# Delta-rule attention feeding a rational MLP: two products of the block inverse and the state's second half on Pool, the second half of the off-diagonal blocks on ACT and PE

## The chip, the cores and the metric

The kernel runs on one core of one Trainium2 chip. The metric is the device time of one launch in microseconds; the kernel before takes 858.86 us, the median of three runs (855.03 to 863.0).

A core has five engines that run their own instruction streams in order and meet at semaphores. In the profile, PE is TensorE (matrix products, results in PSUM; PEld is its weight load), DVE is VectorE, ACT is ScalarE, POOL is GpSimd, and SP is the engine that issues nearly all of this kernel's DMAs.

## The reference, cut to what matters

```python
# delta rule, per batch and head (4 x 8), over 768 tokens of head width 48
k_n = k / (norm(k) + 1e-6)
for t in range(S):
    y[t]  = q[t] @ state
    v_old = k_n[t] @ state
    state = state + beta[t] * outer(k_n[t], v[t] - v_old)
# the 3072 rows of y (8 heads x 48 = 384 wide) then go through an MLP of width 2048
h = x @ w_in
P = a0 + a1*h + a2*h**2 + a3*h**3
Q = 1 + |b0|*|h| + |b1|*h**2
out = (P / (Q + 1e-6)) @ w_out
```

All inputs and the output are float32 (moe_w_in and moe_w_out are float64 and are read as pairs of words).

## The kernel before

**Chunks.** The 768 tokens are cut into 12 chunks of 64. Within a chunk the sequential rule becomes matrix products: the 64x64 matrix of key products, its strictly lower part times beta, a triangular solve against it, one product for the state's update and one for the output. Two batches lie side by side on the 128 partitions, so a tile is 128 partitions by 16 (batch pair, head) combinations by 48 or 64 columns: 768 or 1024 elements per partition.

**Two halves.** Every product on PE runs in float16 with each operand split into a first half (the value rounded to float16) and a second half (the rest, again float16). `split16` makes them: ACT writes the first half, DVE or POOL subtracts it from the source. `mm3` then makes three passes, first by first, second by first, first by second, 48 matrix products in all for the 16 heads.

**The inverse (lines 526 to 594).** The triangular matrix is cut into 16x16 diagonal blocks, which are inverted with elementwise instructions, 128 blocks on 128 partitions at once. It begins with 4x4 blocks, and a loop then joins two 4x4 into 8x8 (n = 4) and two 8x8 into 16x16 (n = 8). Each join is a product of blocks written as an elementwise product (line 564), a sum over the last axis (line 567), a second product (line 569) and a second sum (line 574). For n = 8 each product has 512 elements per partition; for n = 4 there are two of 64. The inverse, times 256, is split into two halves (lines 580 and 581, both on DVE) and goes through DRAM (`img`) to the layout that PE needs (`wc`). There is one buffer of the inverse (`wt`); its diagonal is written by ACT in line 537.

**The off-diagonal blocks (lines 596 to 609).** PE multiplies the key products by the inverse of the diagonal blocks into a PSUM tile `pe`. `split16` makes the two halves of pe / 256 in `et`: ACT the first, DVE the second, from PSUM. Six SP transfers a chunk lay them out as block-diagonal weights `ebd`. The solve (lines 685 to 701) is a product with `wbd` and three steps with `ebd`, each with a split of its own.

**The state (lines 667 to 683 and 703 to 712).** `S16` is the state in float32, updated by DVE in line 708. `state_split` makes its two halves `sh`, scaled by d["ss"]: ACT the first (line 230), DVE the second (line 234). `residual` multiplies the keys with `sh` on PE into `pk`, and DVE subtracts that from v in line 679.

**The MLP.** A chunk's 256 tokens go through the MLP in eight units of 256 hidden columns, 96 units in all. In each, PE makes `ph` (18 products, line 806); ACT, DVE and POOL make numerator, denominator and quotient (lines 823 to 853; ACT takes a logarithm and an exponential to divide, and POOL writes the quotient's second half `mg` in line 853); and PE adds the unit's part of the output in `po` (12 products, line 868).

**The order.** At the start, a list of letters ("fgbwoafagfa") runs through the first chunks' stages, and the weights are loaded, converted from float64 and split. In the main loop, each of a chunk's eight units carries pieces of the attention of later chunks: the solve, state and outputs one chunk ahead (`back`), off-diagonal blocks, state split and residual two ahead (`middle`), key products, inverse and query products three ahead (`front`), loads four ahead (`ahead`). The code's order isn't the final order: a planner simulates the engines with modelled costs and arranges the instructions by that, and `tc.high_priority` lets the solve, the off-diagonal blocks, the state split and the residual go earlier.

**Buffers.** `pe` lies in a PSUM pool with one buffer, which key and query products (`pg`, `pm`) also use. The tag "fq" is one SBUF buffer for the squares of keys, queries and values (lines 464 and 616).

Of the kernel before, what the change touches and what calls it, by code (L numbers as in the profile page):

```python
# [10 lines left out]
F16 = mybir.dt.float16  # L11
F32 = mybir.dt.float32
BF16 = mybir.dt.bfloat16
U32 = mybir.dt.uint32
AF = mybir.ActivationFunctionType
ALU = mybir.AluOpType
# [20 lines left out]
def kernel(  # L37
# [12 lines left out]
    nc = tc.nc  # L50

    B, H, S, D = q.shape
    DM, DFF = moe_w_in.shape
    P = 128
    C = 64
# [7 lines left out]
    HP = NPAIR * H  # L63
# [16 lines left out]
    cpool = ctx.enter_context(tc.tile_pool(name="cpool", bufs=1))  # L80
    sb = ctx.enter_context(tc.tile_pool(name="sb", bufs=2))
# [10 lines left out]
    PAIRS = range(NPAIR)  # L92
# [4 lines left out]
    def mark(nm, c, dma):  # L97
        marks[f"{nm}{c}"] = dma.ins
# [24 lines left out]
    identf = cpool.tile([P, P], F32, name="identf")  # L123
    make_identity(nc, identf)
    ident16 = cpool.tile([P, P], F16, name="ident16")
    nc.vector.tensor_copy(ident16, identf)

    zmask = cpool.tile([P, NB], F32, name="zmask")
    nc.vector.tensor_reduce(
# [5 lines left out]
    nc.gpsimd.memset(ones16, 1.0)  # L135


    mask = cpool.tile([P, C], F32, name="mask")
    nc.gpsimd.memset(mask, 1.0 / 256.0)
    for b in range(2):  # L140
        sl = slice(b * C, (b + 1) * C)
# [34 lines left out]
    def zeroed(n, shape, dtype, nm, part=lambda t: t, eng=nc.gpsimd):  # L176
        made = []
        for i in range(n):
# [14 lines left out]
            eng=nc.vector if nm in "kwe" else nc.gpsimd,  # L193
# [10 lines left out]
    for i in range(NIMG):  # L204
        t = dfix.tile([P, BS], F32, name=f"img{i}")
# [3 lines left out]
    def as_rows(ap, b):  # L209

        return (
            ap[b * C : (b + 1) * C]
            .rearrange("(m j) x -> m (j x)", j=NB)[:, : C * C]
            .rearrange("m (t s) -> t m s", s=C)
        )

    def as_blocks(ap):

        return ap[:, : 16 * C].rearrange("m (i s) -> m i s", s=C)[:, :, :16]

    S16 = cpool.tile([P, HP, D], F32, name="S16")

    def split16(dst, src, scale=None, eng=None, hi=None):

        if hi is not None:
            hi.tensor_scalar(dst[0], src, 1.0 if scale is None else scale, 0.0, op0=ALU.mult, op1=ALU.add)
        elif scale is None:
            nc.scalar.copy(dst[0], src)  # L228
        else:
            nc.scalar.activation(dst[0], src, AF.Copy, scale=scale)  # L230
        if scale is None:
            (eng or nc.vector).tensor_sub(dst[1], src, dst[0])  # L232
        else:
            nc.vector.scalar_tensor_tensor(  # L234
                out=dst[1], in0=src, scalar=scale, in1=dst[0], op0=ALU.mult, op1=ALU.subtract
            )

    def parts(t):
        return t[:, 0], t[:, 1]
# [155 lines left out]
    def mm3(dst, bd, rt, start=True, stop=True):  # L395

        for p in PAIRS:
            mm3p(dst, bd, rt, p, start, stop)
# [13 lines left out]
    def bank(pool, nm, w):  # L412

        t = pool.tile([P, NPAIR, 512], F32, tag="a", name=nm)[:, :, : H * w].rearrange("x p (h w) -> x p h w", w=w)
        return t[:, 0], t[:, 1], t

    def by_pair(t):

        return t.rearrange("x (p h) d -> x p h d", p=NPAIR)

    def parts_by_pair(t):
        return by_pair(t[:, 0]), by_pair(t[:, 1])
# [103 lines left out]
    def inverse(c):  # L526


        d = info[c]
        gb = sb.tile([P, 272], F32, tag="gb", name=f"gb_{c}", bufs=1)  # L530
        dma = nc.sync.dma_start(out=gb[:, :256].rearrange("p (i j) -> p i j", j=16), in_=as_blocks(d.pop("gd")))
        mark("gb", c, dma)
        yield
        wt = wt_b[0]
        pr = sb.tile([P, 512], F32, tag="pr", name=f"pr_{c}", bufs=1)
        xt = sb.tile([P, 64], F32, tag="ab", name=f"ab_{c}", bufs=1)
        nc.scalar.copy(wt[:, 0:256:17], bblk[:, c])

        def blocks(t, n, at, x):

            t = t.rearrange("p (e x) -> p e x", x=x)[:, :, at : at + 16 * n]
            return t.rearrange("p e (i j) -> p e i j", j=16)[..., :n]


        w4 = blocks(wt, 4, 0, 68)
        a4 = xt.rearrange("p (e i j) -> p e i j", e=4, i=4)
        b4 = bblk[:, c].rearrange("p (e i) -> p e i", e=4)
        nc.vector.tensor_mul(a4, blocks(gb, 4, 0, 68), b4.unsqueeze(3).broadcast_to([P, 4, 4, 4]))
        for i in range(1, 4):
            pv = pr[:, : 4 * i * i].rearrange("p (e k j) -> p e k j", e=4, k=i)  # L550
            ai = a4[:, :, i, :i].unsqueeze(2).broadcast_to([P, 4, i, i])
            nc.vector.tensor_mul(pv, w4[:, :, :i, :i], ai)
            nc.vector.tensor_reduce(w4[:, :, :i, i], pv, axis=AX.X, op=ALU.add)

        for n in (4, 8):
            x = 34 * n
            e = 8 // n
            shape = [P, n, n, n]
            w21 = blocks(wt, n, n, x)
            prod = pr[:, : e * n ** 3].rearrange("p (e a b j) -> p e a b j", e=e, a=n, b=n)  # L560
            xs = xt[:, : e * n * n].rearrange("p (e i j) -> p e i j", e=e, i=n)
            g21, w11, w22 = blocks(gb, n, 16 * n, x), blocks(wt, n, 0, x), blocks(wt, n, 17 * n, x)
            for m in range(e):
                nc.vector.tensor_mul(
                    prod[:, m], g21[:, m].unsqueeze(1).broadcast_to(shape), w11[:, m].unsqueeze(2).broadcast_to(shape)
                )
            nc.vector.tensor_reduce(xs, prod, axis=AX.X, op=ALU.add)
            for m in range(e):
                nc.vector.tensor_mul(
                    prod[:, m],  # L570
                    xs[:, m].unsqueeze(2).broadcast_to(shape),
                    w22[:, m].rearrange("p k i -> p i k").unsqueeze(1).broadcast_to(shape),
                )
            nc.vector.tensor_reduce(w21, prod, axis=AX.X, op=ALU.add)
            if n == 4:
                yield
        wtf = wt[:, :256]

        wh = sb.tile([P, 256, 2], F16, tag="wh", name=f"wh_{c}", bufs=1)
        nc.vector.tensor_scalar_mul(wh[..., 0], wtf, 256.0)  # L580
        nc.vector.scalar_tensor_tensor(
            out=wh[..., 1], in0=wtf, scalar=256.0, in1=wh[..., 0], op0=ALU.mult, op1=ALU.subtract
        )
        if c == 0:
            nc.vector.tensor_scalar(
                gate.bitcast(U32), wtf[:, 127:128].bitcast(U32), 0, 897 << 20, op0=ALU.bitwise_and, op1=ALU.bitwise_or
            )
        im = img[c % NIMG]
        words = wh.rearrange("p x i -> p (x i)").bitcast(F32)
        nc.sync.dma_start(out=as_blocks(im), in_=words.rearrange("m (t c) -> m t c", c=16))  # L590
        wc = d["wc"] = sb.tile([P, HP, C, 2], F16, tag="wc", name=f"wc_{c}", bufs=1)
        words = wc.rearrange("p m s i -> p (m s i)").bitcast(F32).rearrange("p (m s) -> p m s", s=C)
        for b in range(2):
            nc.sync.dma_start(out=words[b * C : (b + 1) * C], in_=as_rows(im, b))

    def off_blocks(c):

        d = info[c]
        gbd, wc = d.pop("gbd"), d.pop("wc")
        pe = bank(ps_f, f"pe_{c}", C - 16)  # L600
        mm3(pe, gbd, wc[:, :, 16:])
        d["wbd"] = to_diagonal("w", wc)
        et = sb.tile([P, 2, HP, C - 16], F16, tag="u0", name=f"et_{c}", bufs=1)
        split16(parts_by_pair(et), pe[2], 1.0 / 256.0)
        ebd = d["ebd"] = diag["e"][0]
        for b in range(2):
            for j in range(NB - 1):
                sl = slice(b * C + 16 * j, b * C + 16 * j + 16)
                nc.sync.dma_start(out=ebd[sl, :, :, b, 16 * (j + 1) :], in_=et[sl, :, :, 16 * j :])
# [57 lines left out]
    def state_split(c):  # L667

        d = info[c]
        d["sh"] = sb.tile([P, 2, HP, D], F16, tag="sh", name=f"sh_{c}", bufs=2)  # L670
        split16(parts(d["sh"]), S16, d["ss"])

    def residual(c):
        d = info[c]
# [263 lines left out]
    def middle(c, j):  # L938

        if j == 0:  # L940
            with tc.high_priority(1000):
                info[c]["gbd"] = to_diagonal("w", info[c].pop("gl"))
        elif j == 3:
            with tc.high_priority(300):
                off_blocks(c)
        elif j == 5:
            if c > 0:
                with tc.high_priority(300):
                    state_split(c)
            with tc.high_priority(300):  # L950
                residual(c)
            diagonals(c)
# [53 lines left out]
    for n in range(N + 2):  # L1006
        c, j = divmod(n, NU)
# [38 lines left out]
```

## Time and profile before

| what | value |
|---|---|
| median of 3 runs | 858.86 us (855.03 to 863.0) |
| the profiled execution, its own time | 857.44 us |
| its span, first to last instruction | 855.5 us |
| mean granted TensorE clock | 0.883 |
| instructions | 23235 |

| engine | busy us | share | instructions |
|---|---|---|---|
| PE | 624.5 | 73% | 9264 |
| DVE | 770.2 | 90% | 1369 |
| ACT | 593.4 | 69% | 1242 |
| POOL | 467.6 | 55% | 430 |

How to read the rows that follow. A row of instruction groups gives the line of the code, the engine, the operation, the tile written and the tiles read, the form (partitions by elements, types) and the count; behind the first bar the busy time in us and the mean duration of one in ns; behind the second the time in us that the engine stood idle just before these instructions, and what ended most of it. A row by stage gives the stretch in us from the span's start and then each engine's busy time, with the count of instructions. A row of waits names who waited for whom: us in total, how often, the longest. In a row of one line's durations stand shortest, median and longest in ns, and then the first and last start in us. A line can be that of a helper: 234 and 230 are in `split16`, 403 is in `mm3p`, so the tile's name tells which use it is. PE's busy time is modelled for pipelined products and isn't its peak rate.

### The profile page before, as it was taken

Reading aid. Unit: us, or ns where it says so; the run is one execution under the profiler, and the core shown is the slowest. Engines: PE = TensorE matmul, PEld = TensorE weight load, DVE = VectorE, ACT = ScalarE, POOL = GpSimd, SP = SyncE. Lnnn points to the kernel's source line nnn. Section 1 sums busy time; section 2 is a strip of 40 time slices with the busy share of each in tenths; the row PEclk is TensorE's granted clock in tenths of the full one; section 3 lists DMA queues with packets and bytes.
Section 4 is the critical chain, followed back from the end, with each engine's and each line's share of the span. In section 5 each row is a group of like instructions: output and inputs, shape, how many; then the busy total and the mean of one; then the engine's idle time right before and its main releaser. Section 6 shows DMA issues by size and latency. Waiting matters only on the chain. (4 is left out here: it accounts for less than half of the span.)

```text
span 855.5 us, 23235 instructions
## 1 busy us (share of the span) xinstructions
PE 624.5 (73%) x9264; PEld 491.8 (57%) x9264; DVE 770.2 (90%) x1369; ACT 593.4 (69%) x1242; POOL 467.6 (55%) x430
## 2 busy tenths in 40 slices
PE   0230425865887697598878979888789889999885
PEld 0220424644666376476667757666677667776563
DVE  5999898899889969889899999998999998998896
ACT  4766666865666584685867777767768767887774
POOL 7665655454436345654764855746738455353622
PEclk9755555987899799889989999999989999999998
DMA  8997979966996976878879779579588572300000
GB/s 236 245 202 155 221 148 173 143 137 131 162 158 112 182 142 112 143 148 154 145 139 162 118 147 165 102 148 162 97 169 143 114 114 49 71 2 20 1 19 19
DMA packets 466508, 111.47 MB, mean 130 GB/s; under 512 B 431328, under 2 KB 463072, under 8 KB 466400
## 3 DMA queue, kind: packets, MB, share of 16 engines
q1 hardware_dynamic: 464224, 108.83, 68.5%
q8 instruction: 72, 1.18, 0.6%
q10 hardware_dynamic: 2176, 1.17, 0.4%
q14 instruction: 36, 0.29, 0.1%
HBM read 40.47 MB, written 26.23 MB: 78 GB/s over the span
## 5 line engine op out<-in xcount | busy, mean ns | idle before, releaser
L806 PE MATMUL ph<-xT,w_in 128*128 128x256 f16 x1728 | 225.6, 285 | 39.2 <-DVE mu L830 32.8
L868 PE MATMUL po<-w_out,mg 128*128 128x384 f16 x1152 | 219.0, 337 | 35.0 <-POOL mg L853 31.4
L806 PEld LDWEIGHTS <-w_in 128*128 128x128 f16 x1728 | 173.1, 102 | 76.7 <-DVE mu L830 34.9
L853 POOL TENSOR_TENSOR mg<-mu,mr 128x512 f16<-128x512 f32 x96 | 133.5, 1391 | 132.7 <-DVE mu L852 83.2
L868 PEld LDWEIGHTS <-mg 128*128 128x128 f16 x1152 | 109.3, 100 | 109.7 <-POOL mg L853 41.0
L823 ACT ACTIVATE mu<-ph,coef,msc 128x512 f32<-128x512 f32 x96 | 74.0, 771 | 49.4 <-POOL mg L853 20.2
L829 ACT ACTIVATE mw<-mw 128x512 f32<-128x512 f32 x96 | 60.4, 629 | 55.3 <-DVE mw L828 55.0
L848 DVE SCALAR_TENSOR_TENSOR mw<-mw,msc,mg 128x512 f32<-128x512 f32 x96 | 87.0, 907 | 0.7
L826 DVE TENSOR_TENSOR mu<-ph,mu 128x512 f32<-128x512 f32 x96 | 65.4, 681 | 19.4 <-ACT mr L825 14.0
L850 POOL TENSOR_TENSOR mu<-mu,mw 128x512 f32<-128x512 f32 x36 | 50.3, 1398 | 53.1 <-DVE mw L848 31.2
L403 PEld LDWEIGHTS <-kbd 128*128 128x128 f16 x1680 | 59.8, 102 | 25.5 <-issue 19.1
L828 DVE SCALAR_TENSOR_TENSOR mw<-mr,msc,ph 128x512 f32<-128x512 f32 x96 | 70.5, 735 | 0.0
L830 DVE SCALAR_TENSOR_TENSOR mu<-mu,msc,ph 128x512 f32<-128x512 f32 x96 | 70.4, 734 | 0.0
L841 ACT ACTIVATE mr<-mw,msc 128x512 f32<-128x512 f32 x96 | 69.0, 719 | 1.2
L403 PE MATMUL pu<-z,ebd 128*128 128x48 f16 x1728 | 53.7, 186 | 20.3 <-DVE z L234 14.9
L403 PEld LDWEIGHTS <-ebd 128*128 128x128 f16 x1728 | 52.8, 98 | 22.8 <-issue 21.5
L825 ACT ACTIVATE mr<-ph,msc 128x512 f32<-128x512 f32 x96 | 65.2, 679 | 0.0
L847 DVE SCALAR_TENSOR_TENSOR mg<-mu,msc,mr 128x512 f16<-128x512 f32 x60 | 59.3, 988 | 2.5 <-ACT mr L842 2.5
L842 ACT ACTIVATE mr<-mr 128x512 f32<-128x512 f32 x96 | 60.0, 625 | 1.1
L852 DVE SCALAR_TENSOR_TENSOR mu<-mu,msc,mw 128x512 f32<-128x512 f32 x60 | 55.7, 928 | 0.4
L403 PEld LDWEIGHTS <-wbd 128*128 128x128 f16 x1152 | 38.6, 101 | 28.3 <-issue 27.1
L232 POOL TENSOR_TENSOR mm<-m,mm 128x1024 f16<-128x1024 f32 x12 | 31.7, 2639 | 34.2 <-ACT mm L228 34.2
(198 smaller groups left out, 1313.7 us busy)
## 6 DMA issues: line engine op xcount, KB each, us to landing
wsi<-in_moe_w_in_dram SPq DMA_DIRECT2D x24, 256.0 KB, 5.2
xdk<-kn SPq DMA_DIRECT2D x24, 256.0 KB, 3.6
kbd<-tk SPq DMA_DIRECT2D x24, 256.0 KB, 4.5
gd<-g SPq DMA_DIRECT2D x24, 256.0 KB, 3.8
wso<-in_moe_w_out_dram SPq DMA_DIRECT2D x32, 192.0 KB, 3.8
xdq<-kn SPq DMA_DIRECT2D x24, 256.0 KB, 3.4
mbd<-mm SPq DMA_DIRECT2D x24, 256.0 KB, 5.8
wc<-img SPq DMA_DIRECT2D x24, 256.0 KB, 5.3
```

Of the source, the lines that this page charges most:

```text
L403: nc.tensor.matmul(dst[p][:, h], head(bd, lp, p * H + h), head(rt, rp, p * H + h), start=start and n == 0 and h == 0, stop=stop and n == l ...
L806: nc.tensor.matmul(ph[:, i], w_in[:, f2, wp, cc, i * P : (i + 1) * P], x[:, xp, cc], start=k == 0, stop=k == 3 * NCC - 1,)
L823: nc.scalar.activation(u, ph, AF.Identity, scale=A3, bias=a2)
L825: nc.scalar.activation(z, ph, AF.Abs, scale=B1)
L826: nc.vector.tensor_mul(u, ph, u)
L828: nc.vector.scalar_tensor_tensor(out=w, in0=z, scalar=B0, in1=ph, op0=ALU.add, op1=ALU.mult)
L829: nc.scalar.activation(w, w, AF.Abs)
L830: nc.vector.scalar_tensor_tensor(out=u, in0=u, scalar=A1, in1=ph, op0=ALU.add, op1=ALU.mult)
L841: nc.scalar.activation(r, w, AF.Ln, bias=Q0)
L848: nc.vector.scalar_tensor_tensor(out=w, in0=w, scalar=Q0, in1=g[:, 0], op0=ALU.add, op1=ALU.mult)
L853: nc.gpsimd.tensor_mul(g[:, 1], u, r)
L868: nc.tensor.matmul(po[p], g[:, gp, i, p * P : (p + 1) * P], w_out[:, f2, wp, i], start=f2 == lo and i == 0 and k == 0, stop=f2 == hi - 1 a ...
```

## The change

1. The two elementwise products of the inverse go from DVE to POOL for n = 8 (two of 512 elements a chunk); for n = 4 they stay on DVE, as do all sums.
2. The inverse's first half (`wh`, line 580) is made by ACT instead of DVE.
3. In the off-diagonal blocks, ACT writes the first half as before; PE then adds -256 times that half to `pe`, as a product with a constant matrix (-256 on the diagonal), one for each of the two batch pairs; and ACT scales what is left by 1/256 into the second half. The DVE instruction goes.
4. The state's second half: ACT writes the scaled state to a float32 tile `st` (in the buffer "fq"), and POOL subtracts the first half from it. The DVE instruction goes.
5. A new constant tile `minus256`, made once; the causal mask (0 and 1/256) becomes bfloat16.

```diff
@@ constants
+    minus256 = cpool.tile([P, P], F16, name="minus256")
+    nc.vector.tensor_scalar(minus256, identf, -256.0, None, op0=ALU.mult)
-    mask = cpool.tile([P, C], F32, name="mask")
+    mask = cpool.tile([P, C], BF16, name="mask")
@@ inverse
+            eng = nc.vector if n == 4 else nc.gpsimd
             for m in range(e):
-                nc.vector.tensor_mul(
+                eng.tensor_mul(
                     prod[:, m], g21[:, m].unsqueeze(1).broadcast_to(shape), w11[:, m].unsqueeze(2).broadcast_to(shape)
                 )
             nc.vector.tensor_reduce(xs, prod, axis=AX.X, op=ALU.add)
             for m in range(e):
-                nc.vector.tensor_mul(
+                eng.tensor_mul(
                     prod[:, m],
                     xs[:, m].unsqueeze(2).broadcast_to(shape),
                     w22[:, m].rearrange("p k i -> p i k").unsqueeze(1).broadcast_to(shape),
...
-        nc.vector.tensor_scalar_mul(wh[..., 0], wtf, 256.0)
+        nc.scalar.activation(wh[..., 0], wtf, AF.Copy, scale=256.0)
@@ off_blocks
-        split16(parts_by_pair(et), pe[2], 1.0 / 256.0)
+
+        for i in range(2):
+            nc.scalar.activation(parts_by_pair(et)[i], pe[2], AF.Copy, scale=1.0 / 256.0)
+            for p in PAIRS if i == 0 else ():
+                nc.tensor.matmul(
+                    pe[p].rearrange("x h t -> x (h t)"),
+                    minus256,
+                    et[:, 0, p * H : (p + 1) * H].rearrange("x h t -> x (h t)"),
+                    start=False,
+                    stop=True,
+                    skip_group_check=True,
+                )
@@ state_split
-        split16(parts(d["sh"]), S16, d["ss"])
+        hi, lo = parts(d["sh"])
+        nc.scalar.activation(hi, S16, AF.Copy, scale=d["ss"])
+        st = sb.tile([P, HP, D], F32, tag="fq", name=f"st_{c}", bufs=1)
+        nc.scalar.activation(st, S16, AF.Copy, scale=d["ss"])
+        nc.gpsimd.tensor_sub(lo, st, hi)
```

## The prediction, on record before the result

> **What bounds the kernel now.** I read the page first (busy shares, slices), then busy time by stage, then the waits, then the costs of the forms that the change touches.
>
> ```profile
> span 855.5 us, 23235 instructions
> ...
> PE 624.5 (73%) x9264; PEld 491.8 (57%) x9264; DVE 770.2 (90%) x1369; ACT 593.4 (69%) x1242; POOL 467.6 (55%) x430
> ...
> DVE  5999898899889969889899999998999998998896
> ```
>
> DVE is busy 90% of the span, and its slices are 8 or 9 nearly everywhere. By stage:
>
> ```profile
> core 0: us, PE busy (x) PEld busy (x) DVE busy (x) ACT busy (x) POOL busy (x), PEclk, DMA share, GB/s
> 160.00:250.00 90.00, 62.22 (x908) 47.52 (x905) 85.41 (x144) 58.74 (x127) 44.03 (x35) 0.87 0.78 143
> 250.00:400.00 150.00, 117.06 (x1927) 94.04 (x1928) 129.21 (x213) 96.69 (x193) 75.64 (x66) 0.90 0.79 144
> 400.00:600.00 200.00, 169.96 (x2661) 134.87 (x2658) 187.25 (x303) 148.38 (x296) 125.16 (x100) 0.96 0.83 144
> ...
> sum 695.00, PE 571.75 PEld 445.82 DVE 631.94 ACT 489.64 POOL 371.58; mean PE 114.35 PEld 89.16 DVE 126.39 ACT 97.93 POOL 74.32
> ```
>
> Here 400 to 600 us is the middle of the run: DVE 187 of 200, PE 170 (at granted clock 0.96), ACT 148, POOL 125. The sum is that of 160 to 855 us. The waits say the same:
>
> ```profile
> POOL mg L853 <- DVE mu L852: 83.2, 28, 8.2
> ...
> ACT mw L829 <- DVE mw L828: 55.0, 46, 3.3
> ...
> PEld L806 <- DVE mu L830: 34.9, 12, 5.8
> ...
> PE po L868 <- POOL mg L853: 31.4, 28, 3.2
> ```
>
> The others wait for DVE; PE also waits for POOL's L853, which itself waits for DVE. So DVE's work sets the pace, and PE is second, 17 us behind in 200.
>
> **The change: what DVE loses.** Five groups leave it, whole:
>
> ```profile
> L569 DVE TENSOR_TENSOR pr<-ab,wt 128x512 f32<-128x512 f32 x12 | 16.7, 1390 | 0.0
> ...
> L234 DVE SCALAR_TENSOR_TENSOR sh<-S,sc,sh 128x768 f16<-128x768 f32 x11 | 13.2, 1200 | 0.0
> ...
> L234 DVE SCALAR_TENSOR_TENSOR et<-pe,et 128x768 f16<-128x768 f32 x12 | 11.4, 949 | 1.9 <-ACT et L230 1.2 <-DMA tq<-xdq 0.7
> ...
> L564 DVE TENSOR_TENSOR pr<-gb,wt 128x512 f32<-128x512 f32 x12 | 11.0, 918 | 0.0
> ...
> L580 DVE TENSOR_SCALAR wh<-wt 128x256 f16<-128x256 f32 x12 | 8.7, 722 | 0.0
> ```
>
> 16.7 + 13.2 + 11.4 + 11.0 + 8.7 = 61.0 us. Part of that is not work. The next rows show the two products undisturbed and a DVE instruction caught behind a POOL one (from the instructions in order of time: start and duration in us), and the spread of the conversion and of the state's split (shortest, median, longest in ns):
>
> ```profile
> 505.37 0.68 DVE L564 TENSOR_TENSOR pr<-gb,wt 128x512 f32<-128x512 f32 x1
> ...
> 511.49 1.02 DVE L569 TENSOR_TENSOR pr<-ab,wt 128x512 f32<-128x512 f32 x1
> ...
> 525.65 2.13 DVE L852 SCALAR_TENSOR_TENSOR mu<-mu,msc,mw 128x512 f32<-128x512 f32 x1
> ```
> ```profile
> 524.41 2.83 POOL L232 TENSOR_TENSOR mm<-m,mm 128x1024 f16<-128x1024 f32 x1 [0.18 <-ACT mm L228]
> ```
> ```profile
> L580 DVE TENSOR_SCALAR wh<-wt x12: 293/374/1743, 71.6 to 694.9; 128x256 f16<-128x256 f32 x12
> ```
> ```profile
> L234 DVE SCALAR_TENSOR_TENSOR sh<-S,sc,sh x11: 1001/1008/2045, 130.6 to 735.5; 128x768 f16<-128x768 f32 x11
> ```
>
> L852 began inside POOL's product and ended 0.54 us after it (527.78 against 527.24): it seems to have stood until POOL was done. Undisturbed, the five cost 12 x (0.68 + 1.02 + 0.95 + 0.29) + 11 x 1.00 = 46.3 us. The other 14.7 us are waits for POOL, and may simply pass to the next DVE instruction that needs what POOL holds; I let half pass, 7.3 us (bounds 0 and 14.7).
>
> **What POOL gains, and what that costs DVE.** The trace has no such product on POOL; the nearest rows:
>
> ```profile
> L850 POOL TENSOR_TENSOR mu<-mu,mw 128x512 f32<-128x512 f32 x36 | 50.3, 1398 | 53.1 <-DVE mw L848 31.2 <-ACT mr L825 5.9 <-ACT sf L764 3.3
> ...
> L232 POOL TENSOR_TENSOR rr<-v,rr 128x768 f16<-128x768 f32 x12 | 22.5, 1874 | 11.7 <-ACT rr L228 11.7
> ...
> L505 POOL TENSOR_TENSOR k<-k,nrm 128x768 f32<-128x768 f32 x12 | 18.4, 1532 | 10.8 <-DVE nrm L504 9.4 <-DVE vss L364 1.1 <-DMA gd<-g 0.4
> ```
>
> 24 products at L850's 1.40 (same size and types) and 11 subtractions at 1.87 make 33.6 + 20.6 = 54 us. Below: L505 scaled to 512 elements, 1.02, gives 45. Above: the second product reads its last factor with a step, and costs DVE 1.02 / 0.68 = 1.5 times the first; if POOL pays that too, 12 x 0.7 more, 63. I take 54: POOL goes from 468 to 522, some 63% of a shorter span.
>
> What a POOL microsecond costs DVE comes from the instructions whose two operands are both SBUF tiles, against L828 and L826, which read PSUM for one:
>
> ```profile
> L848 DVE SCALAR_TENSOR_TENSOR mw<-mw,msc,mg 128x512 f32<-128x512 f32 x96 | 87.0, 907 | 0.7
> ...
> L847 DVE SCALAR_TENSOR_TENSOR mg<-mu,msc,mr 128x512 f16<-128x512 f32 x60 | 59.3, 988 | 2.5 <-ACT mr L842 2.5
> L852 DVE SCALAR_TENSOR_TENSOR mu<-mu,msc,mw 128x512 f32<-128x512 f32 x60 | 55.7, 928 | 0.4
> L845 DVE TENSOR_TENSOR mg<-mu,mr 128x512 f16<-128x512 f32 x36 | 37.8, 1050 | 8.2 <-ACT mr L842 8.0 <-POOL mu L834 0.2
> ```
> ```profile
> L828 DVE SCALAR_TENSOR_TENSOR mw<-mr,msc,ph x96: 725/735/743, 153.6 to 840.5; 128x512 f32<-128x512 f32 x96
> ```
> ```profile
> L826 DVE TENSOR_TENSOR mu<-ph,mu x96: 630/681/693, 152.9 to 839.9; 128x512 f32<-128x512 f32 x96
> ```
> ```profile
> L848 DVE SCALAR_TENSOR_TENSOR mw<-mw,msc,mg x96: 656/743/2294, 160.4 to 844.8; 128x512 f32<-128x512 f32 x96
> ```
>
> L828 never leaves 725 to 743 ns; L848 has the same median and goes to 2294. The excess is 96 x 0.172 + 60 x 0.253 + 60 x 0.193 + 36 x 0.369 = 56.6 us, over 371.6 us of POOL: 0.15 us of DVE for each of POOL. The new 54 us cost DVE 8.2 (bounds: nothing, if they fall beside PSUM readers, and all 54, if each meets such an instruction at its start).
>
> The Trainium skill, "SBUF — State Buffer", section "Who interferes with whom", states that a DVE instruction with two SBUF inputs and a GpSimd instruction that reads SBUF exclude each other for the whole instruction, whoever starts second blocking fully. By that rule the upper bound of 54 is the whole price of the move; the trace agrees on the kind of wait (the 2.13 us of L852) but shows the average at 0.15.
>
> **New handoffs.** DVE's 24 reductions (L567, L574 for the 8-wide step) now wait for POOL, and 12 L581 for ACT; behind them on DVE stand the MLP instructions. Nearest is L845 behind ACT's L842, in the row above: 8.2 us idle over 36, so 0.23 each, 36 x 0.23 = 8.2 us. A lower end is 0.2 us in all, what L845 waited for POOL's L834; an upper one is 1 us each, 36.
>
> POOL's products wait for DVE, and L853 is queued behind them, with PE's po behind that. The rows nearest to what ACT and PE gain:
>
> ```profile
> L868 PE MATMUL po<-w_out,mg 128*128 128x384 f16 x1152 | 219.0, 337 | 35.0 <-POOL mg L853 31.4 <-DVE mg L847 2.2 <-DVE mg L845 1.1
> ...
> L230 ACT ACTIVATE sh<-S,sc 128x768 f16<-128x768 f32 x11 | 10.2, 929 | 2.8 <-DVE S L708 2.7
> ...
> L318 ACT ACTIVATE wai<-wsi 128x256 f32<-128x256 f32 x24 | 10.1, 427 | 2.6 <-DVE w_out L320 2.5
> ...
> L230 ACT ACTIVATE et<-pe 128x768 f16<-128x768 f32 x12 | 9.6, 801 | 2.6 <-PE pe L403 2.6
> ```
>
> ACT gains 12 x 0.80 (second et) + 11 x 0.93 (st) + 12 x 0.43 (wh) = 24.9 us, to 618. PE gains 24 products of 128x384 at 219.0 / 1152 = 0.19, 4.6 us. Both stand between other work, on engines with idle time; I cost them at nothing on the path. Without that cover, et would reach its six SP transfers, and any transfer queued behind those, 0.19 x 2 + 0.80 - 0.95 = 0.2 us later a chunk, 3 us in all. st takes the buffer of the squares, so ACT's next square waits for POOL's subtraction. The bf16 mask and the constant matrix I cost at nothing: L658 reads PSUM, and one small instruction is added at the start. No DMA is added.
>
> **The sum.** DVE: 61.0 - 7.3 - 8.2 - 8.2 = 37 us, 3.1 a chunk. How much reaches the span depends on PE:
>
> ```profile
> L679 DVE SCALAR_TENSOR_TENSOR v<-v,sc,pk x11: 997/1001/1015, 149.6 to 740.4; 128x768 f32<-128x768 f32 x11
> ```
> ```profile
> who waited for it (us, times):
> ...
>   PE pk L403: 0.6, 1
> ```
>
> Ten chunks take 590.8 us, 59.1 each, so 200 us hold 3.4 chunks and DVE falls from 187 to 177 there, PE rising to 171. Two engines that feed each other and are that close don't both stay full; I let a third of the relief turn into idle time: 37 x 2/3 = 25 us. The profiled execution's own time is 857.44, so 832.4; the median of the runs shown is 858.86, 1.4 above it. Forecast: 834 us. Its own range is 819 to 849: three quarters of 61.0 - 8.2 - 0.2 = 52.6 us come through, or half of the 20 that are left if all 14.7 pass on and a handoff costs 0.5 (61.0 - 14.7 - 8.2 - 18).
>
> **Rivals.**
>
> *The relief in full.* Nothing passes on, handoffs are cheap, PE keeps up: the 52.6 us, about 806. For it: PE has 30 us free in 200. Against it: DVE and PE would then be at 172 and 171 there. Chance 0.12.
>
> *The relief is swallowed.* With 1 us for each of 36 handoffs, 61.0 - 7.3 - 8.2 - 36 = 9.5 us are left, and two thirds of it 6: about 853, anywhere from 849 to 866. For it: a DVE stall is paid at once, as DVE has no slack. Against it: L845's row shows 0.23 for such a handoff. Chance 0.21.
>
> *The state comes late: slower.* pk on PE waits for the state's second half, and everything of the MLP queued on PE behind it waits too. DVE's 1.20 becomes 0.93 on ACT, 1.87 on POOL, and a stand behind L853 at POOL's head, 83.2 / 28 = 3.0: 4.6 us more for each of 11 chunks, 51 us, against 25 gained: about 885. It decides from 2.3 us a chunk (25 / 11). Against it: pk waited for sh 0.6 us in the whole run (last row above, from the list of who waited for the tile sh). Chance 0.10.
>
> *POOL holds DVE in full: slower.* 54 + 14.7 + 8.2 - 61.0 = 16 us lost, about 875; it decides from (61.0 - 14.7 - 8.2) / 54 = 0.7 us of DVE for each of POOL, against 0.15 measured. Chance 0.04.
>
> **How the numbers follow.** 0.53 is left for the forecast. 1% is about what a measurement of this kernel can tell from no change, 850.3 to 867.5. Faster: 0.12 + 0.53 = 0.65. Within: 0.21. Slower: 0.10 + 0.04 = 0.14. The range leaves out the slower cases and half of the full relief: 808 to 866.
>
> **What would show it.** DVE's busy time falls by about 45 us (61.0 less 7.3 and 8.2), to some 725; L848, L847, L852 grow by a tenth or less; ACT near 618, POOL near 522; idle time before L567 and L574 stays near 0.23 us each; PE's pk waits for POOL stay under 2 us a chunk; DVE's share in the middle falls a little while PE's rises. Wrong if DVE's busy time hardly falls (the waits passed on), if DVE is idle before the reductions by a microsecond each, or if POOL's idle time before L853 vanishes and PE's po waits grow past 50 us.

## The result, and the profile after

The changed kernel takes 870.75 us (median of four runs, 870.71 to 871.12) against 858.79 before (four runs): 1.0138 times as long, with a 95% interval of 1.0104 to 1.0171. The prediction was 834 and faster. The profiled execution took 871.12 us, its span is 869.4.

The page of the changed kernel (the lines that answer to those of before):

```profile
span 869.4 us, 23275 instructions
...
PE 631.0 (73%) x9288; PEld 496.0 (57%) x9288; DVE 735.0 (85%) x1311; ACT 615.0 (71%) x1277; POOL 514.0 (59%) x465
...
DVE  5997698787699597859989689899889999889896
```

The work moved about as forecast: DVE 770 to 735, ACT 593 to 615, POOL 468 to 514, PE 625 to 631. But DVE's idle time rose from 855.5 - 770.2 = 85 us to 869.4 - 735.0 = 134 us. The 35 us that left it and 14 more turned into standing still. By stage (us of the stretch, busy time and instructions of each engine, granted clock, share and rate of DMA):

```profile
160.00:250.00 90.00, 68.52 (x1023) 53.54 (x1021) 68.82 (x134) 63.49 (x133) 51.99 (x41) 0.87 0.85 153
250.00:400.00 150.00, 117.33 (x2004) 93.70 (x2005) 120.25 (x192) 101.72 (x201) 88.81 (x73) 0.94 0.86 146
400.00:600.00 200.00, 159.82 (x2477) 127.23 (x2475) 178.09 (x275) 144.38 (x285) 131.90 (x106) 0.94 0.82 139
```

Between 400 and 600 us DVE went from 187 to 178, as the prediction had it (177). PE was to rise to 171 and fell from 170 to 160, ACT from 148 to 144: the stretch holds less work of every engine but POOL. Nothing took DVE's place as the fullest engine. The groups on DVE (busy, mean ns, then the idle time before it and what ended it):

```profile
L866 DVE SCALAR_TENSOR_TENSOR mw<-mw,msc,mg 128x512 f32<-128x512 f32 x96 | 94.5, 987 | 0.8
...
L844 DVE TENSOR_TENSOR mu<-ph,mu 128x512 f32<-128x512 f32 x96 | 65.4, 682 | 26.5 <-ACT mr L843 24.4 <-issue 1.6 <-POOL mu L852 0.5
L865 DVE SCALAR_TENSOR_TENSOR mg<-mu,msc,mr 128x512 f16<-128x512 f32 x60 | 63.9, 1066 | 10.9 <-ACT mr L860 9.2 <-PE po L886 1.6
...
L584 DVE SCALAR_TENSOR_TENSOR wh<-wt,wh 128x256 f16<-128x256 f32 x12 | 12.9, 1077 | 1.0 <-ACT sw L282 1.0
...
L570 DVE TENSOR_REDUCE ab<-pr 128x64 f32<-128x512 f32 x12 | 8.1, 678 | 3.3 <-POOL pr L567 3.3
L577 DVE TENSOR_REDUCE wt<-pr 128x64 f32<-128x512 f32 x12 | 8.1, 676 | 1.1 <-POOL pr L572 1.1
```

The rows of before that answer to L844 and L584:

```profile
L826 DVE TENSOR_TENSOR mu<-ph,mu 128x512 f32<-128x512 f32 x96 | 65.4, 681 | 19.4 <-ACT mr L825 14.0 <-issue 1.9 <-POOL mg L853 1.6
...
L581 DVE SCALAR_TENSOR_TENSOR wh<-wt,wh 128x256 f16<-128x256 f32 x12 | 5.6, 468 | 0.0
```

The new handoffs are cheap: the sums wait 3.3 + 1.1 = 4.4 us for POOL in all. The new idle time lies elsewhere. Two thirds of it ended with a result of ACT (DVE's idle time ended by ACT went from 52 to 85 us), spread over many instructions: in front of MLP instructions that the change doesn't touch (L844 waits for ACT 24.4 us, 14.0 before; L865 9.2, 2.5 before) and in front of the attention's. L584, which the change leaves on DVE, went from 468 to 1077 ns: it now takes the waits for POOL that L580 had taken (p_wh, below, bears this out).

### The profile page after: what moved, and what is told of

It reads as the page before. It is cut to its first block, busy times and chain, and to the rows that moved or that the text cites. A ratio compares the mean times of both kernels' runs of the same rounds, so it can differ in the third digit from the quotient of the medians.

```text
span 869.4 us, 23275 instructions
## 1 busy us (share of the span) xinstructions
PE 631.0 (73%) x9288; PEld 496.0 (57%) x9288; DVE 735.0 (85%) x1311; ACT 615.0 (71%) x1277; POOL 514.0 (59%) x465
## 4 chain that ended last, share of the span: by engine, by line
DVE 29%; ACT 17%; DMA 16%; PE 13%; issue 8%; POOL 8%; SPq 8%; ACTq 0%; POOLq 0%; DVEq 0%
PE ph L824 5%; PE po L886 4%; DVE mw L866 4%; DVE mg L865 3%; DVE mu L844 3%; DMA k<-in_k_dram 2%; DVE mw L846 2%; DVE w_out L329 2%; ACT mu L841 2%; ACT mr L843 2%; SPq L119 2%; DVE mu L848 2%; POOL mg L871 2%; DMA tk<-xdk 2%; DMA gb<-gd 2%
## 5 line engine op out<-in xcount | busy, mean ns | idle before, releaser
L886 PE MATMUL po<-w_out,mg 128*128 128x384 f16 x1152 | 220.5, 336 | 34.1 <-POOL mg L871 29.4
L871 POOL TENSOR_TENSOR mg<-mu,mr 128x512 f16<-128x512 f32 x96 | 130.6, 1362 | 102.6 <-DVE mu L870 78.2
L847 ACT ACTIVATE mw<-mw 128x512 f32<-128x512 f32 x96 | 60.4, 629 | 55.7 <-DVE mw L846 55.5
L866 DVE SCALAR_TENSOR_TENSOR mw<-mw,msc,mg 128x512 f32<-128x512 f32 x96 | 94.5, 987 | 0.8
L844 DVE TENSOR_TENSOR mu<-ph,mu 128x512 f32<-128x512 f32 x96 | 65.4, 682 | 26.5 <-ACT mr L843 24.4
L405 PEld LDWEIGHTS <-kbd 128*128 128x128 f16 x1680 | 62.6, 105 | 24.3 <-issue 22.8
L865 DVE SCALAR_TENSOR_TENSOR mg<-mu,msc,mr 128x512 f16<-128x512 f32 x60 | 63.9, 1066 | 10.9 <-ACT mr L860 9.2
L870 DVE SCALAR_TENSOR_TENSOR mu<-mu,msc,mw 128x512 f32<-128x512 f32 x60 | 59.8, 998 | 0.6
L405 PEld LDWEIGHTS <-ebd 128*128 128x128 f16 x1728 | 51.4, 98 | 15.5 <-issue 13.5
L405 PEld LDWEIGHTS <-wbd 128*128 128x128 f16 x1152 | 34.7, 99 | 39.3 <-issue 37.9
L852 POOL TENSOR_SCALAR mu<-mu,msc 128x512 f32<-128x512 f32 x36 | 29.1, 808 | 36.1 <-DVE mu L848 25.3
```

What stands on the lines that cost most here:

```text
L405: nc.tensor.matmul(dst[p][:, h], head(bd, lp, p * H + h), head(rt, rp, p * H + h), start=start and n == 0 and h == 0, stop=stop and n == l ...
L844: nc.vector.tensor_mul(u, ph, u)
L865: nc.vector.scalar_tensor_tensor(out=g[:, 0], in0=u, scalar=A0, in1=r, op0=ALU.add, op1=ALU.mult)
L866: nc.vector.scalar_tensor_tensor(out=w, in0=w, scalar=Q0, in1=g[:, 0], op0=ALU.add, op1=ALU.mult)
L871: nc.gpsimd.tensor_mul(g[:, 1], u, r)
L886: nc.tensor.matmul(po[p], g[:, gp, i, p * P : (p + 1) * P], w_out[:, f2, wp, i], start=f2 == lo and i == 0 and k == 0, stop=f2 == hi - 1 a ...
```

## The experiments

Two theories were set against each other. WORK: what the change adds to ACT and POOL, or makes later, costs the time. ORDER: the planner answers any edit with another order of most instructions, and the order is what costs. The finished streams give a reason to suspect it: of the 1310 instructions on DVE that both kernels have, the longest sequence that stands in the same order in both traces has 792.

**Twelve one-element copies; another priority.**

```diff
     def off_blocks(c):
         d = info[c]
+        nc.scalar.copy(speck, consts[:, 0:1])     # n_act_speck
-            with tc.high_priority(300):            # n_prio, the step off_blocks
+            with tc.high_priority(320):
```

> The kernel before with one ACT copy of one element per partition added in each chunk's off-diagonal step (12 in all, about 0.2 us each by the one-element copy of line 626, so 2.4 us of ACT work). The planner answers with another order of most instructions. Theory ORDER (the order that the planner happens to find is worth a per cent or more, and the change's 1.4% is mostly that): this moves by 1% or more, either way. Theory WORK (what the change puts on ACT and POOL, or makes later, costs the time): this stays within 0.5% of the kernel before, 855 to 863.

> The kernel before with the off-diagonal step's priority 320 in place of 300: no instruction is added, removed or moved to another engine, only the planner's order differs. ORDER: 1% or more off the kernel before, either way, and not the same as the other order variants. WORK: within 0.5%.

n_act_speck: 876.36 us, 1.0225 [1.0191, 1.0258]. Twelve ACT instructions that compute nothing and whose result nothing reads cost 18 us, more than the whole change. The trace shows where the planner put them (shortest, median, longest in ns, first and last start in us):

```profile
L601 ACT COPY speck<-consts x12: 174/191/192, 2.1 to 13.7; 128x1 f32<-128x1 f32 x12
```

All twelve ran in the first 14 us, 2.3 us of work in all and far ahead of the main loop, so they can't have held up the off-diagonal steps for which they were written. n_prio: 859.9 us, 1.0023 [0.9993, 1.0053], with single runs from 854.7 to 866.8. So a new order alone can be worth over 2%, and needn't be. WORK's 0.5% is missed in the first, ORDER's 1% in the second.

**The planner's simulation off.** One word in the context, for both kernels:

```diff
-    with _tile.TileContext(nc, schedule_with_timeline_sim=True) as tc:
+    with _tile.TileContext(nc, schedule_with_timeline_sim=False) as tc:
```

> The kernel before with the planner's simulation of the engines turned off, so that the instructions keep the order of the code and its priorities. It is the base for the next run. Both theories: slower than the kernel before, by an amount that neither gives; DVE still the busiest engine.

> The changed kernel with the planner's simulation turned off. Its order is that of the previous run but for the instructions that the change itself moves. ORDER: faster than the previous run by 2 to 4% of it, as 61 us of DVE work leave and nothing is shuffled. WORK: slower than the previous run by about 1%, or equal.

1148.37 us without the change and 1168.58 with it, 1.8% more. ORDER expected 2 to 4% less and missed; WORK expected about 1% more or no difference, and had the way right and the size too small. But this order is a third slower than the planner's and no engine is near full in it: DVE, still the busiest, is busy for 65% of the time without the change and 62% with it, so an emptier DVE has little to earn there. It shows that the change isn't faster in this order; it doesn't show what it is worth in an order in which DVE is nearly full.

**The parts alone, freely ordered.** Each kernel is before with one of the change's edits.

> The kernel before with the two 512-element products of the inverse on POOL, and nothing else. DVE loses 27.7 us of busy time, POOL gains about 37 (1.71 and 1.41 us each in the changed kernel). WORK: the four parts alone add up to about the whole, +12 us, each of them between 0 and +8. ORDER: each part alone lands anywhere within 2.5% of the kernel before, and the four do not add up to +12.

> The kernel before with the new off-diagonal step (second half by a product on PE and by ACT), the constant matrix and the bf16 mask. DVE loses 11.4 us, ACT gains 9.6. WORK: 0 to +8 us. ORDER: anywhere within 2.5%.

> The kernel before with the new state step alone (scaled copy on ACT, subtraction on POOL). DVE loses 13.2 us, ACT gains 10.2, POOL 18.3. The rival of the prediction, that the state comes late, expects this part to carry the loss: +10 us or more, with PE waiting for the state's second half. ORDER: anywhere within 2.5%, and no such wait.

> The kernel before with the first half of the inverse made by ACT instead of DVE, 12 instructions of 256 elements. DVE loses 8.7 us, ACT gains about 5. WORK: within 0.5% of the kernel before. ORDER: anywhere within 2.5%.

| part | us | ratio, 95% |
|---|---|---|
| e_inv | 873.87 | 1.0180 [1.0136, 1.0224] |
| e_off | 867.54 | 1.0114 [1.0080, 1.0148] |
| e_state | 860.02 | 1.0019 [0.9998, 1.0040] |
| e_wh | 862.69 | 1.0057 [1.0035, 1.0079] |

Against the kernel before of these runs (857.36) that is 16.5 + 10.2 + 2.7 + 5.3 = 35 us, where the whole lost 12. WORK expected the parts to add up, each between 0 and +8 us, and ORDER expected them not to: the two largest lie above WORK's bound, and the sum is three times the whole. The state, which the prediction had as its first rival on the slow side, costs next to nothing.

**The order held.** The next kernels separate the two. At the end of the trace, edges that fix only the order of issue, and make nothing wait for a result, tie each instruction to the one that stood ahead of it on its engine (or on SP's queue) in the finished order of another kernel. Instructions that only one of the two has are left to the planner. The code is shortened here:

```diff
         tile_delta_rule__then__rational_moe_kernel(tc, *args)
+        traced = list(tc.nc.cur_bb.bb.instructions)
+        for at in ORDER:      # per engine: places in the trace, in the finished order of the other kernel
+            for a, b in zip(at[:-1], at[1:]):
+                tc.add_manual_dep(traced[b], traced[a].name, NO_SYNC, reason="pinned")
```

> The changed kernel's work in the order of the kernel before: edges that only fix the order hold every instruction that both kernels have, on all engines and on SP's queue, in the place that it has before; only the new instructions are put in by the planner. ORDER: with the order out of the way the 35 us less of DVE work show, 835 to 850. WORK: slower than the kernel before by 1% or more, 867 or above. In between, 851 to 866: the work itself is worth nothing either way.

> The work of the kernel before in the order of the changed kernel, held in the same way. ORDER: the slower order costs it what it costs the changed kernel or more, 871 to 890. WORK: it stays at the kernel before's time, 855 to 863, without the change's work.

q_before, which does none of the change's work, takes 873.01 us, 1.0170 [1.0143, 1.0197]. In its trace all 1310 DVE instructions that the changed kernel also has stand in that kernel's order. In the changed kernel's order the old work is as slow as the new (870.75). The two run side by side. Here is the same instruction of the middle chunk, DVE's split of the tokens, in the changed kernel, in q_before and in before (start and duration in us):

```profile
546.08 1.02 DVE L236 SCALAR_TENSOR_TENSOR xT<-px,sf,xT 128x768 f16<-128x768 f32 x1 [1.31 <-ACT xT L232]
```
```profile
546.91 1.02 DVE L234 SCALAR_TENSOR_TENSOR xT<-px,sf,xT 128x768 f16<-128x768 f32 x1 [1.31 <-ACT xT L230]
```
```profile
532.78 1.00 DVE L234 SCALAR_TENSOR_TENSOR xT<-px,sf,xT 128x768 f16<-128x768 f32 x1
```

Even the wait of 1.31 us ahead of it is the same in the first two. All twelve of these splits, one a chunk (first and last start at the end of the first part of the row), in the same three kernels:

```profile
L236 DVE SCALAR_TENSOR_TENSOR xT<-px,sf,xT x12: 1000/1017/1018, 137.3 to 810.5; 128x768 f16<-128x768 f32 x12
```
```profile
L234 DVE SCALAR_TENSOR_TENSOR xT<-px,sf,xT x12: 1001/1014/1018, 138.4 to 813.1; 128x768 f16<-128x768 f32 x12
```
```profile
L234 DVE SCALAR_TENSOR_TENSOR xT<-px,sf,xT x12: 1005/1010/1019, 144.5 to 798.1; 128x768 f16<-128x768 f32 x12
```

From the first to the last it is 673.2 us in the changed kernel, 674.7 in q_before and 653.6 before. So the new order loses 20 us in the main loop, and its start, which is 7 us shorter, gives some of it back. The page of q_before:

```profile
span 870.1 us, 23217 instructions
...
PE 630.0 (72%) x9264; PEld 496.0 (57%) x9264; DVE 768.3 (88%) x1369; ACT 593.0 (68%) x1242; POOL 463.3 (53%) x430
```

DVE does 33 us more here than in the changed kernel, ACT 22 less and POOL 51 less, and the span is the same within a microsecond. So in this order neither the relief nor the new work shows, and the order that the planner found for the change is enough by itself for the 12 us that were lost. That is ORDER's half. Its other half fell: p_after, the new work in the old order, takes 878.03 us, 1.0233 [1.0208, 1.0257], which is what WORK expected. The two losses don't add up: 14 us for the new order alone, 19 for the new work alone, 12 for both. The parts were then held in the old order one by one.

> The two products of the inverse on POOL alone, in the order of the kernel before. Freely ordered, this part was slower by 1.8%. ORDER: the same as the kernel before or faster by up to 15 us. WORK: slower again, by 1% or more.

> The new state step alone, in the order of the kernel before. Freely ordered, it took 0.2% more than the kernel before. ORDER: 0 to 8 us faster. WORK, by the prediction's rival of a late state: slower by 4 us or more, with PE waiting for the state's second half, as the products with the state stand where they stood.

> The new off-diagonal step alone (with the constant matrix and the bf16 mask), in the order of the kernel before. If this part carries the whole's loss there: 10 to 19 us slower, with PE or ACT waiting between the first half, the product and the second half. If the loss is of the parts together: within 4 us of the kernel before.

> The first half of the inverse on ACT alone, in the order of the kernel before. ACT would stand until DVE's last sum of the inverse is done, with the MLP behind it (11.9 us of such idle time in the whole change held in this order). If this part carries the loss: 10 us slower or more. If not: within 4 us.

| part, in before's order | us | ratio, 95% | DVE busy (before 770.2) |
|---|---|---|---|
| p_inv | 857.46 | 0.9980 [0.9954, 1.0006] | 752.5 |
| p_state | 860.98 | 1.0022 [1.0001, 1.0043] | 769.5 |
| p_wh | 857.26 | 0.9986 [0.9960, 1.0012] | 769.0 |
| p_off | 875.63 | 1.0213 [1.0170, 1.0257] | 761.3 |

p_inv lost 1.8% when it was ordered freely and loses nothing here: that loss was order. Three of the parts are worth nothing either way; p_state's 2 us more lie between its two expectations, outside both. The off-diagonal step carries p_after's whole loss. The last column holds a second lesson: p_wh takes 8.7 us from DVE and its busy time falls by 1.2; p_state takes 13.2, gives POOL 20 more, and it falls by 0.7.

**DVE relieved, and nothing put in its place.** This asks the prediction's main premise directly, in the held order and freely. The tiles that are no longer fully written get buffers of their own, zeroed at the start, so nothing waits for the missing instructions. The diff shows one of the five places.

```diff
-        split16(parts(d["sh"]), S16, d["ss"])        # likewise et; wh[..., 0] and the two products: left out
+        nc.scalar.activation(parts(d["sh"])[0], S16, AF.Copy, scale=d["ss"])
```

> The kernel before, in its own order, without the five groups of DVE instructions that the change takes away and with nothing in their place: the two 512-element products of the inverse, the first half of the inverse and the second halves of the off-diagonal blocks and of the state are left out (what reads them reads zeros or older values). DVE BINDS (the prediction): 40 to 55 us faster, 804 to 819. COUPLED (the engines wait for each other in a fixed order, and none alone sets the pace): faster by under 20 us, above 839, with DVE idle in place of the work.

> The same work left out, with the order free to the planner. DVE BINDS: 40 to 55 us faster, whatever the order adds or takes (up to 2.5%). COUPLED: between 835 and 870, the order's scatter around a small gain.

p_relief: 849.92 us, 0.9906 [0.9874, 0.9939]. e_relief: 842.82 us, 0.9822 [0.9782, 0.9863]. Both lie where COUPLED put them and far from the 804 to 819 of a binding DVE. p_relief's page, and its wait in front of the MLP's first DVE instruction:

```profile
span 848.2 us, 23157 instructions
...
PE 621.6 (73%) x9264; PEld 490.8 (58%) x9264; DVE 726.6 (86%) x1310; ACT 593.0 (70%) x1242; POOL 464.1 (55%) x435
```
```profile
L829 DVE TENSOR_TENSOR mu<-ph,mu 128x512 f32<-128x512 f32 x96 | 65.6, 683 | 40.0 <-ACT mr L828 24.9 <-POOL mm L236 9.4 <-issue 3.3
```

DVE's busy time fell by 770.2 - 726.6 = 43.6 us and the span by 855.5 - 848.2 = 7.3; the other 36.3 became idle time (848.2 - 726.6 = 121.6, from 85.3). One sixth reached the span. Most of that isn't even in the main loop: the first split of the tokens starts at 139.9 us instead of 144.5, and from there to the last it is 651.3 us instead of 653.6. In the free order (DVE 717.5 us, span 840.8) 14.7 of 52.7 us reached the span. Ahead of that MLP instruction the idle time went from 19.4 us to 40.0, mostly for ACT.

**Why the off-diagonal step costs in the old order.** In p_off, the instructions of ACT in order of time around one chunk's step:

```profile
504.25 0.79 ACT L608 ACTIVATE et<-pe 128x768 f16<-128x768 f32 x1
...
507.62 0.68 ACT L838 ACTIVATE mr<-ph,msc 128x512 f32<-128x512 f32 x1
508.19 0.78 ACT L836 ACTIVATE mu<-ph,coef,msc 128x512 f32<-128x512 f32 x1
508.85 0.70 ACT L838 ACTIVATE mr<-ph,msc 128x512 f32<-128x512 f32 x1
509.42 1.07 ACT L895 ACTIVATE ob<-po,kp 128x384 f32<-128x384 f32 x2
510.35 0.84 ACT L608 ACTIVATE et<-pe 128x768 f16<-128x768 f32 x1
```

and of PE:

```profile
502.82 3.81 PE L881 MATMUL po<-w_out,mg 128*128 128x384 f16 x20
506.47 0.49 PE L610 MATMUL pe<-et,minus 128*128 128x384 f16 x2
```

The new product stands behind 20 of the MLP's on PE, the second half behind ACT's MLP work, and it is done 6.9 us after the first half began (511.19 less 504.25). Before, the same chunk's first half began at 493.31 and DVE was done at 496.82, 3.5 us (over all twelve chunks the mean is 5.3 us in p_off and 2.8 before):

```profile
493.31 0.79 ACT L230 ACTIVATE et<-pe 128x768 f16<-128x768 f32 x1
```
```profile
495.87 0.95 DVE L234 SCALAR_TENSOR_TENSOR et<-pe,et 128x768 f16<-128x768 f32 x1
```

Until then the six transfers to `ebd` wait, and `pe`'s one PSUM buffer is held: 6.8 us a chunk before, 8.9 in p_off, 4.8 in p_relief, from its first product to its last reader. The waits that p_off's expectation named are hardly there, since both engines have other work in between: ACT stood for the new product 1.6 us in the whole run and the product for ACT 1.2. Two runs tested this account: one leaves out only the second half, the other sets the new product 14 places behind the last product into `pe` and the second half directly behind the first.

> The kernel before, in its own order, with only the second half of the off-diagonal blocks left out (11.4 us of DVE work; what reads it reads zeros). HELD TILE (the time for which pe is held sets the loss and the gain): most of the 7 to 8 us that leaving out all five groups gained, 849 to 853. DVE WORK (each microsecond off DVE is worth the same): 11.4 / 61 of that gain, 1.4 us, 855 to 859.

> The new off-diagonal step alone, in the order of the kernel before, but with its two products 14 places behind the last product into pe on PE (directly behind in the first chunk) and its second half directly behind the first on ACT. Before, PE took up to 20 products and ACT five instructions in between. HELD TILE: pe is held for less than 8.9 us a chunk and most of the 18 us come back, 857 to 866. If the step costs by its work on ACT and PE, or by PE's and ACT's standing for each other: 872 or more.

p_off_early: 865.87 us, 1.0084 [1.0053, 1.0114], so 11 of the 18 us come back with the same work; that is the upper edge of HELD TILE's range. In the chunk that answers to the one above, the second half is now done 2.2 us after the first began (495.79 less 493.63; the mean over the chunks is 2.4, less than before):

```profile
493.63 0.79 ACT L608 ACTIVATE et<-pe 128x768 f16<-128x768 f32 x1
494.98 0.81 ACT L608 ACTIVATE et<-pe 128x768 f16<-128x768 f32 x1 [0.57 <-PE pe L610]
```

The place of the two instructions is worth more than half of the step's cost. The rest isn't settled: `pe` is held for 6.3 us there, less than before, and the kernel is still 7 us slower; PE now stands 11.4 us in all for ACT's first half and ACT 9.3 us for PE's product. p_noet: 855.28 us, 0.9967 [0.9940, 0.9993], in the range of DVE WORK and outside that of HELD TILE, though it holds `pe` for only 4.3 us. The gain, 2.8 us by the ratio and 0.6 to 5.2 by its interval, is too small to separate the two finely. But the held tile alone doesn't set the time: q_before holds it for 5.5 us a chunk, less than before, and is 14 us slower.

## Why the prediction was wrong

**"DVE's work sets the pace" failed.** This is the step. The rows that it stood on were right: DVE was busy for 90%, and waits for DVE were the longest. But busy for 90% in this kernel isn't the same as binding. Taking 61 us of work away, with nothing added, gained 7.2 us in the same order (849.92 against 857.16) and 14.3 in a free one (842.82). The sum let two thirds of the relief through; measured, it is a sixth of what the busy time fell by in the held order, and 14.7 / 52.7, just over a quarter, in the free one. What was read as DVE keeping the others waiting fits each engine, in an order fixed beforehand, waiting for another in turn: with work taken off it, DVE stood for longer ahead of the same MLP instruction (19.4 to 40.0 us in p_relief).

**The order was left out.** No term of the sum and no rival held that the planner would arrange the kernel anew, though the prediction's front matter describes the planner. It is as large as any effect that these runs found: q_before loses 14 us to the new order without any of the new work, n_act_speck 18 us by twelve copies. Of the six freely ordered edits other than the relief (two empty ones and four parts), none was faster than before, and they lie from +0.2% to +2.2%.

**The new work on ACT and PE was put at nothing.** The prediction covered the off-diagonal step's product and second copy with idle time of their engines, and without that cover counted 0.2 us a chunk, 3 us in all. In the old order the step costs 18.5 us (p_off), and the second half is done 5.3 us after the first began instead of 2.8. What was left out is where the two instructions stand in their queues; placed earlier they cost 7 us (p_off_early). In the changed kernel's own order this cost doesn't show, since the old work is as slow there.

**What the prediction had right.** Nearly every sign that it named came, and none of its three signs of being wrong: DVE's busy time fell, DVE stood only 4.4 us ahead of the sums, and PE's po waits for POOL went from 31.4 to 29.4 us. Only PE's share in the middle, which was to rise, fell. These signs watch the sizes of the terms; none of them asks whether DVE binds. DVE's busy time, 725 forecast and 735 measured; ACT 618 and 615; POOL 522 and 514. Handoffs: 0.23 us each forecast for the sums behind POOL, 4.4 / 24 = 0.18 measured. POOL's products: 1.40 forecast, and measured:

```profile
L572 POOL TENSOR_TENSOR pr<-ab,wt 128x512 f32<-128x512 f32 x12 | 20.5, 1712 | 3.7 <-DVE ab L570 3.7
...
L689 POOL TENSOR_TENSOR sh<-st,sh 128x768 f16<-128x768 f32 x11 | 18.3, 1668 | 0.7 <-ACT st L688 0.5
...
L567 POOL TENSOR_TENSOR pr<-gb,wt 128x512 f32<-128x512 f32 x12 | 16.9, 1411 | 26.2 <-DVE wt L577 25.7 <-DVE sw L255 0.5
```

The product that reads with a step takes 1.71, between the 1.40 taken and the 2.1 of the upper end; together 55.7 us against 54.

**DVE's waits for POOL were undersized.** 61.0 us left DVE and its busy time fell by 35.2, so 25.8 came back where 7.3 + 8.2 = 15.5 had been set. L584 alone took 12 x 0.61 = 7.3 of it, and L866, L865 and L870 grew by 7 to 9% each, 16.6 us together. The Trainium skill, "SBUF — State Buffer", section "Who interferes with whom", states a rule that fits: DVE instructions with two SBUF inputs and GpSimd instructions that read SBUF exclude each other. p_wh agrees: the one-input conversion left, and the two-input L581 behind it went from 468 to 832 ns:

```profile
L581 DVE SCALAR_TENSOR_TENSOR wh<-wt,wh 128x256 f16<-128x256 f32 x12 | 10.0, 832 | 0.0
```

Five of these twelve took 0.86 to 1.82 us, and each of the five ended 0.3 us after a POOL instruction that had begun before it. Two others kept to 0.43 us although a POOL instruction had begun 0.4 us before them and went on past their end, so the wait isn't met every time. L580 itself, with one SBUF input, had waited in the same way: before, its six long instances (0.43 to 1.74 us) each ended 0.17 us after such a POOL instruction. The prediction passed half of the removed waits on; in p_wh 4.4 of L580's 5.2 us of waiting (12 x 0.43, over its undisturbed 0.29) came back at L581 (12 x 0.364).

**The rivals.** That the state comes late didn't happen: in the held order this part costs 0.2%, and in the changed kernel no product with the state waits for its second half (of those who waited for the tile, only DVE's L697 stands in the list, with 1.8 us). POOL holding DVE in full didn't happen either: 26 us, not 69, came back. Its time, about 875, lies close to the measured 870.75 by luck, since its mechanism isn't there. The full relief is refuted by p_relief. The swallowed relief (849 to 866) lies nearer than the forecast, also by the wrong mechanism: its handoffs of 1 us each were measured at 0.18.

**What stays open.** Which loop through the engines sets the pace in before's order, and why the planner's order for the changed kernel is slower, were not found. p_after wasn't repeated with the off-diagonal step's instructions placed early, so what the whole change is worth in the old order at its best isn't known. The 14 us of e_relief hold one draw of the order's scatter, which reached 18 us. Nor was it tried whether the order of the kernel before is an unusually good one among many.

## What to carry to other kernels

Before a relief is priced, ask whether the engine binds: leave the work out, put nothing in its place, hold the order, and look at whether its idle time grows by what its busy time falls. Where a planner arranges the instructions, an edit is two changes, the work and a new order; run the old work in the new order (and an edit that does nothing) before the difference is put down to the work. A new instruction between two others on a path is placed in two queues, and where it stands there can cost more than it takes.

## What the runs showed that wasn't expected

Twelve one-element ACT copies in the first 14 us made the kernel 2.2% slower, through the order of everything behind them. Taking a conversion of 0.72 us a chunk off DVE (p_wh) took 0.1 us a chunk off its busy time, since the instruction behind it then met POOL instead. And three parts that move 50 us of DVE's work to POOL and ACT (27.7 + 13.2 + 8.7) can each be made in the old order without moving the time by more than 0.3%.
